# Spacing of the weight conversions in the gated MLP's second pass, and two ordering edges

## The chip, the cores and the metric

The kernel runs on one core of a Trainium2 chip. The metric is the device time of one execution in microseconds (us), taken as the median of several. TensorE (PE) multiplies, with its weight loads shown as PEld; ScalarE (ACT) and VectorE (DVE) do the elementwise work; SyncE (SP) issues nearly all transfers. Each of these engines runs its own instruction list in order. PSUM holds matmul results in eight banks, SBUF holds everything else.

## The reference

```python
attn_out = _attn_ref(q, k, v)          # causal window of 64, 4 x 8 heads x 576 tokens x 64
x = attn_out.transpose(0, 2, 1, 3).reshape(2304, 512)
# gated MLP: 512 -> 1536 -> 512
xn = x / np.sqrt(np.mean(x * x, axis=-1, keepdims=True) + 1e-6) * rms_g
g = xn @ w_gate
x2 = g / (1 + np.exp(-g)) * (xn @ w_val) @ w_out
# second MLP: 512 -> 2048 -> 512
h = x2 @ w_in2
out = h / (1 + np.exp(-1.702 * h)) @ w_out2
```

The weights arrive as 64-bit floats, and the kernel makes 32-bit floats of them itself.

## The kernel before

**Stages.** The 2304 tokens are six blocks of 384. A first pass goes over the six blocks with the first half of the hidden columns of the gated MLP, and does the attention of later blocks in between. A second pass goes over three super-blocks (`sb` 0 to 2) of two blocks with the other half of the hidden columns. Then comes the second MLP, the gelu stage. Each float32 matmul is done as three matmuls on a high and a low part.

**The second pass.** A matrix product of it is a Winograd scheme: seven products of half size for each pair of blocks. One hidden column pair makes one `chain` (line 1020) of seven steps; a step (`prod`) is six matmuls with 384 columns. There are six chains in a super-block, n even for the gate and n odd for the value. A chain works in two PSUM banks, a and b. Steps 0, 1 and 2 each end with `snap` (line 1038), a copy of the bank to SBUF on ACT; steps 3, 4 and 5 end with `plus`, an addition on DVE; step 6 is read from its bank. Later steps go on in the same bank, so that PE may begin step 2 only when the copy of step 0 is done, step 3 when that of step 1 is done, and step 4 when that of step 2 is done. The results go through `gated` (line 1265, Silu on ACT) or `valued` (line 1269, a product on DVE, a cast on ACT at line 1273, the low part on DVE at line 1274). After the chains, `out_units` multiply with the output weights and add to what the first pass left.

**Order.** PE's order is written out by hand. In the second pass each piece of work has a key; super-block `sb` begins at key 50·sb, chain n of it has its steps at keys 7n, 7n+2, ..., 7n+12, and from key 7 on two chains alternate, so that one key is about one step. In the first pass, pieces hang on a count of matmuls (`at_tick`). ACT, DVE and SP are not ordered by hand: a planner with a simulated clock places their instructions, by order of the source among those that it takes to be ready, and may place them well ahead of the work around them. `with after(ins)` adds an edge: what the block issues on the engine of `ins` stands behind `ins`. `hold[0]` is the ACT instruction, `hold_v[0]` the DVE instruction, that was noted last.

**Conversions.** `w_order` lists pairs of weight tiles. Six gate and value pairs of the second half are converted in the first pass by `conversion()` (line 1117); then come three pairs of output weights ("o"), eight pairs of the second MLP's first matrix ("h", all wanted in the gelu stage) and eight of its second ("p"). The "o" and "h" pairs are converted in the second pass by `w_step` (line 240): two ACT instructions on the loaded tile `st` (lines 253 and 254, behind `hold[0]`), two on DVE (255 and 256), then the load of the next pair (`w_load`, line 135). The following `w_step`, or a `w_half` at its own key, finishes the pair: an "o" is split into high and low part (lines 236 and 237); an "h" gets four differences (206 to 209), the high part on ACT (214), the low part on DVE (216) and two stores to DRAM (225, 226). The pool `stp` has three slots of 8 KB a partition for `st` and for the result `m`.

**Transfers.** All go through SP's one queue: weight tiles of a chain (`t_load`, line 1012, 896 KB each, two a chain, the tile freed by an earlier chain), the pairs to be converted (1 MB), the stores of converted pairs, and the next super-block's input (`x_raws`, line 983). `x_steps` (line 986) makes the seven operands `xop` of a super-block out of that input (DVE 1001, ACT 1003, DVE 1004), seven pieces at keys 48.05 and up.

Of the kernel before, what the change touches and what calls it, by code (L numbers as in the profile page):

```python
# [9 lines left out]
F32 = mybir.dt.float32  # L10
# [31 lines left out]
def window_attention__gated_mlp__mlp_kernel(  # L42
# [554 lines left out]
    if True:  # L597
# [382 lines left out]
        def x_raws(src):  # L980
            r = [wp.tile([128, KC, TB], F32, tag="w", name="xr") for _ in range(2)]
            for e in range(2):
                nc.sync.dma_start(out=r[e], in_=src(e))
            return r

        def x_steps(r, ops, hold_on=()):
            a11, a12, a21, a22 = r[0][:, 0:2, :], r[0][:, 2:4, :], r[1][:, 0:2, :], r[1][:, 2:4, :]
            subs = [
                (0, None, a11), (6, (a21, a11, a21, ALU.subtract), a21), (5, (a21, a22, a21, ALU.subtract), a21),
                (4, (a11, a11, a21, ALU.add), a11), (2, (a21, a12, a21, ALU.subtract), a21), (1, None, a12), (3, None, a22),  # L990
            ]

            def step(i, total, src):
                with ExitStack() as es:
                    for ins in hold_on:
                        es.enter_context(after(ins))
                    make(i, total, src)

            def make(i, total, src):
                if total:  # L1000
                    nc.vector.tensor_tensor(*total)  # L1001
                t = x1p.tile([128, 2, 2, TB], F32R, tag="xop", name="xop")
                nc.scalar.copy(t[:, 0], src)  # L1003
                nc.vector.tensor_tensor(t[:, 1], src, t[:, 0].bitcast(F32), ALU.subtract)
                ops[i] = t

            return [lambda a=a: step(*a) for a in subs]

        def t_load(key):
            w = [wp.tile([128, 7, 256], F32R, tag="w", name="wt") for _ in range(2)]  # L1010
# [9 lines left out]
        def chain(n, load, ops, take):  # L1020
            w, xo = load(), ops

            def prod(ps, i, first):
                k = 0
                for wi, xi in ((0, 0), (1, 0), (0, 1)):
                    for c in range(2):
                        on_pe(
                            nc.tensor.matmul,
                            ps[:, :TB],
                            w[wi][:, W_OF["g"][i], c * 128:(c + 1) * 128],  # L1030
                            xo[i][:, xi, c, :],
                            start=(first and k == 0),
                            stop=(k == 5),
                            skip_group_check=not first,
                        )
                        k += 1

            def snap(ps):
                t = small("sn")
                nc.scalar.copy(t, ps[:, :TB])  # L1040
                return t

            def plus(t, ps):
                nc.vector.tensor_tensor(t, t, ps[:, :TB], ALU.add)  # L1044
                return t

            a = bank(n, 0)
            prod(a, 0, True)
            s1 = snap(a)
            yield  # L1050
            b = bank(n, 1)
            prod(b, 6, True)
            s7 = snap(b)
            yield
            prod(a, 5, False)
            s2 = snap(a)
            yield
            prod(b, 3, False)
            take(2, plus(s2, b))
            yield  # L1060
            prod(a, 4, False)
            take(3, plus(s7, a))
            yield
            b = bank(n, 1)
            prod(b, 1, True)
            take(0, plus(s1, b))
            yield
            prod(a, 2, False)
            take(1, a[:, :TB])
            yield  # L1070
# [3 lines left out]
        def put(key, fn):  # L1074
            items.append((key, len(items), fn))
# [32 lines left out]
        def evict(j, acc):  # L1108
            for c in range(KC):
# [4 lines left out]
                    nc.scalar.mul(st, acc[c][:, :T], 0.5)  # L1114
                nc.sync.dma_start(out=osd[j // 2][:, c, (j % 2) * TB:(j % 2 + 1) * TB], in_=st)

        def conversion():
            env = {}

            def first():  # L1120
                w_load(w_next[1] + 1)
                env["key"] = w_order[w_next[1]][0]
                w_next[1] += 1
                st = staged.pop(0).rearrange("p e (f two) -> p (e f) two", two=2)
                env["lo"], env["up"] = lo, hi = st[:, :, 0], st[:, :, 1]
                with after(hold[0]):
                    nc.scalar.activation(hi.bitcast(F32), hi.bitcast(F32), AF.Prelu, scale=2.0 ** -112, alpha=-(2.0 ** 32))

            def second():
                lo, hi = env["lo"], env["up"]  # L1130
                env["mt"] = mt = stp.tile([128, 2, 1024], I32, tag="st", name="m")
                with after(hold[0]):
                    nc.scalar.activation(lo, lo.bitcast(U32), AF.Copy, scale=2.0 ** -29)
                with after(hold_v[0]):
                    nc.vector.tensor_scalar(mt[:, 1, :].bitcast(U32), hi.bitcast(U32), 3, None, ALU.logical_shift_left)

            def add():
                m = env["mt"][:, 1, :]
                with after(hold_v[0]):
                    nc.vector.tensor_tensor(m, m, env["lo"], ALU.add)  # L1140
                with after(last_hop[0]):
                    w_load(w_next[1] + 1)

            def differences():
                env["t"] = t = env["mt"].bitcast(F32).rearrange("p e (b c) -> p (e b) c", c=256)
                b11, b21, b22, b12 = (t[:, 4 + i] for i in range(4))
                with after(hold_v[0]):
                    nc.vector.tensor_tensor(t[:, 0], b12, b11, ALU.subtract)
                    nc.vector.tensor_tensor(t[:, 1], b22, t[:, 0], ALU.subtract)
                    nc.vector.tensor_tensor(t[:, 2], b22, b12, ALU.subtract)  # L1150
                    nc.vector.tensor_tensor(t[:, 3], b21, t[:, 1], ALU.subtract)

            def upper(a, b):
                if a == 0:
                    env["hi"] = wp.tile([128, 7, 256], F32R, tag="w", name="whi")
                with after(hold[0]):
                    nc.scalar.copy(env["hi"][:, a:b], env["t"][:, a:b])

            def lower(a, b):
                hi, m = env["hi"][:, a:b], env["t"][:, a:b]  # L1160
                with after(hold_v[0]):
                    nc.vector.tensor_tensor(m.bitcast(F32R), m, hi.bitcast(F32), ALU.subtract)
                if b == 7:
                    key = env["key"]
                    d = dram.tile([128, 2, 7, 256], F32, name="w%s_%d" % key, tag="w%s_%d" % key)
                    wd[key] = d
                    with after(last_hop[0]):
                        nc.sync.dma_start(out=d[:, 0], in_=env["hi"].bitcast(F32))
                        nc.sync.dma_start(out=d[:, 1], in_=env["t"][:, 0:7])

            return [
                first, second, add, differences,
                lambda: upper(0, 4), lambda: lower(0, 4), lambda: upper(4, 7), lambda: lower(4, 7),
            ]

        for pieces in [[462,474,480,512,516,522,524,529],[562,574,582,588,678,683,687,693],[728,736,743,778,782,788,792,798],[894,900,906,910,942,946,950,954],[959,964,970,976,982,988,992,998],[1004,1010,1016,1022,1034,1040,1044,1048]]:
            for t, fn in zip(pieces, conversion()):
                at_tick(t, fn)
        evict(0, accs)
# [81 lines left out]
        def gated_chains(sb):  # L1261
# [7 lines left out]
            def valued(p, q, c):  # L1269
                t = a4[p, q]  # L1270
                nc.vector.tensor_tensor(t, t, c, ALU.mult)
                g[p, q] = u = gp.tile([128, 2, TB], F32R, tag="g", name="g")
                nc.scalar.copy(u[:, 0], t)
                nc.vector.tensor_tensor(u[:, 1], t, u[:, 0].bitcast(F32), ALU.subtract)

            for i, p in enumerate(ZIG[sb]):
                for k, fn in enumerate((gated, valued)):
# [46 lines left out]
        def put_units(start, units, room):  # L1324
# [3 lines left out]
                key += n if key >= room[0] and key < room[1] else 2  # L1328
            return key

        for sb in range(NSB):
            chains, g = gated_chains(sb)
            put_chains(t0, chains)
            for at_key in [[2.5, 10, 17.5, 25, -32], [6, 16, 26, -36], [2.5, 11, 20, 29, -36]][sb]:
                put(t0 + abs(at_key), w_half if at_key < 0 else lambda: w_step(n_wi))
            for i, (n, fn) in enumerate(out_units(sb, g)):
                if i < 3:
                    key = t0 + 42.2 + 2 * i
# [6 lines left out]
            all_ops[sb + 1] = nops  # L1345
            nsrc = (lambda e, sb=sb: xd[2 * sb + 2 + e]) if sb + 1 < NSB else (lambda e: x2d[0][:, :, e * TB:(e + 1) * TB])
            box = []
            put(t0 + 36.5, lambda nsrc=nsrc, nops=nops, box=box: box.extend(x_steps(x_raws(nsrc), nops)))
            for i in range(7):
                put(t0 + 48.05 + 0.1 * i, lambda box=box: box.pop(0)())  # L1350
            if sb + 1 == NSB:
# [238 lines left out]
```

## Time and profile before

| | |
|---|---|
| three runs | 907.08, 908.44, 909.31 us, median 908.44 |
| the profiled execution | 909.66 us, of which 907.9 us from first to last instruction |
| TensorE clock granted | 1.000 on average |
| PE busy | 898.5 us of 907.9 |
| second pass | from about 328 to 540 us |

The span is what the rows below measure; the 1.8 us around it belong to the execution and stand in every time. A matmul's end is modelled, so PE's progress is read from the starts of its groups.

### The profile page before, as it was taken

How to read it: one execution, taken by the hardware profiler on the slowest of the kernel's cores; microseconds unless marked ns; L12 is line 12 of the kernel's file. 1: busy time of each engine (PE TensorE's matmuls, PEld its weight loads, DVE VectorE, ACT ScalarE, POOL GpSimd, SP SyncE). 2: the span in 40 equal slices, each digit the busy share in tenths (PEclk: the TensorE clock that was granted, in tenths of full speed). 3: DMA queues.
4: the chain of work that ended last, by engine and by line, in shares of the span. 5: the costliest groups of instructions: out<-in, count | busy, mean ns of one | idle time of the engine just before them, and what ended most of it. 6: DMA issues, size and time to landing. Idle time of an engine off the chain costs nothing.

```text
span 907.9 us, 16654 instructions
## 1 busy us (share of the span) xinstructions
PE 898.5 (99%) x6458; PEld 867.5 (96%) x6458; DVE 602.8 (66%) x1237; ACT 509.3 (56%) x1026; POOL 12.9 (1%) x39
## 2 busy tenths in 40 slices
PE   9999999999999999999999999999999999999998
PEld 8999999999999999999999998889899999999998
DVE  5998657777688747937867896656633488234753
ACT  6896656646475356626726657565545455245442
POOL 2000000000000000000000000000000000000000
PEclk9999999999999999999999999999999999999999
DMA  9987576978958859559889989898697778767851
GB/s 205 244 246 216 167 186 197 257 215 236 285 169 312 320 200 344 193 199 376 336 269 354 389 310 381 315 329 294 203 354 263 278 285 310 249 250 262 324 204 53
DMA packets 159407, 240.04 MB, mean 264 GB/s; under 512 B 81248, under 2 KB 131424, under 8 KB 155744
## 3 DMA queue, kind: packets, MB, share of 16 engines
q1 hardware_dynamic: 158800, 238.97, 79.0%
q8 instruction: 51, 0.84, 0.4%
q14 instruction: 28, 0.23, 0.1%
q10 hardware_dynamic: 528, 0.00, 0.0%
HBM read 167.64 MB, written 59.24 MB: 250 GB/s over the span
## 4 chain that ended last, share of the span: by engine, by line
PE 87%; DMA 4%; DVE 4%; ACT 3%; issue 1%; SPq 0%; ACTq 0%; DVEq 0%
PE acc L115 21%; PE psa L115 17%; PE psb L115 13%; PE acca L115 7%; PE psg L115 6%; PE psv L115 5%; PE accb L115 5%; PE ps_warm L121 2%; PE psg L121 1%; PE acc L121 1%; PE psv L121 1%; DMA xr<-x 1%; DMA st<-in_moe_w_in_dram 1%; PE ps_v L115 1%; PE ps_s L115 1%
## 5 line engine op out<-in xcount | busy, mean ns | idle before, releaser
L115 PE MATMUL psa<-xop,wt 128*128 128x384 f32 x1008 | 192.8, 335 | 0.7 <-ACT sn L1040 0.7
L115 PEld LDWEIGHTS psa<-xop,wt 128*128 128x128 f32 x1008 | 176.5, 188 | 3.8 <-ACT sn L1040 1.1
L115 PE MATMUL psb<-xop,wt 128*128 128x384 f32 x756 | 147.2, 335 | 2.7 <-ACT sn L1040 2.4
L115 PEld LDWEIGHTS psb<-xop,wt 128*128 128x128 f32 x756 | 132.5, 188 | 5.7 <-ACT sn L1040 3.0
L1044 DVE TENSOR_TENSOR sn<-sn,psb 128x384 f32<-128x384 f32 x84 | 46.2, 550 | 69.9 <-PE psb L115 68.6
L115 PE MATMUL acc<-g,w 128*128 128x384 f32 x432 | 78.1, 334 | 0.0
L115 PEld LDWEIGHTS acc<-g,w 128*128 128x128 f32 x432 | 75.2, 188 | 0.0
L115 PE MATMUL acca<-wo,sop 128*128 128x256 f32 x576 | 72.0, 283 | 0.3 <-DVE sop L1398 0.3
L1398 DVE TENSOR_TENSOR sop<-g,sop 128x768 fp32r<-128x768 f32 x56 | 53.3, 957 | 28.5 <-ACT sop L1397 28.3
L115 PEld LDWEIGHTS acca<-wo,sop 128*128 128x128 f32 x576 | 70.8, 191 | 0.5 <-DVE sop L1398 0.5
L1040 ACT COPY sn<-psa 128x384 f32<-128x384 f32 x84 | 40.0, 477 | 55.6 <-PE psa L115 55.6
L1397 ACT CAST sop<-g 128x768 fp32r<-128x768 f32 x56 | 46.5, 838 | 40.5 <-PE accb L115 21.7
L115 PE MATMUL acc<-whi,g 128*128 128x512 f32 x192 | 67.8, 392 | 0.0
L1374 ACT ACTIVATE g<-sn 128x384 f32<-128x384 f32 x48 | 25.3, 527 | 52.1 <-DVE sn L1044 52.1
L115 PE MATMUL accb<-wo,sop 128*128 128x256 f32 x432 | 52.8, 283 | 0.0
L115 PEld LDWEIGHTS accb<-wo,sop 128*128 128x128 f32 x432 | 52.3, 192 | 0.0
L1003 ACT CAST xop<-xr 128x768 fp32r<-128x768 f32 x42 | 34.0, 836 | 30.8 <-DVE xr L1001 25.8
L115 PE MATMUL acc<-ah,w 128*128 128x384 f32 x240 | 50.8, 342 | 0.0
L115 PE MATMUL psg<-xh,w 128*128 128x384 f32 x240 | 50.1, 342 | 0.6 <-DVE a L1205 0.5
L115 PE MATMUL psv<-xh,w 128*128 128x384 f32 x240 | 50.3, 340 | 0.0
L420 ACT ACTIVATE p<-p,sm 128x128 f32<-128x128 f32 x96 | 37.5, 393 | 17.1 <-DVE sm L408 17.1
L115 PEld LDWEIGHTS psg<-xh,w 128*128 128x128 f32 x240 | 41.4, 188 | 2.3 <-DVE a L1205 1.2
(204 smaller groups left out, 1565.0 us busy)
## 6 DMA issues: line engine op xcount, KB each, us to landing
wt<-wh SPq DMA_DIRECT2D x48, 896.0 KB, 6.5
wo<-wp SPq DMA_DIRECT2D x28, 1024.0 KB, 6.8
st<-in_moe_w_out_dram SPq DMA_DIRECT2D x28, 512.0 KB, 8.1
wt<-wg SPq DMA_DIRECT2D x14, 896.0 KB, 7.4
wt<-wv SPq DMA_DIRECT2D x14, 896.0 KB, 8.2
xr<-x SPq DMA_DIRECT2D x12, 768.0 KB, 7.2
wh<-whi SPq DMA_DIRECT2D x8, 896.0 KB, 8.3
wh<-m SPq DMA_DIRECT2D x8, 896.0 KB, 9.9
```

The lines of the kernel that those rows point to most:

```text
L115: ins = op(*args, **kw)
L121: ins = op(*args, **kw)
L420: last_exp[0] = nc.scalar.activation(p[e][:, hp, :], p[e][:, hp, :], AF.Exp, bias=sm[:, 0, i:i + 1], scale=-1.0, accum_out=sm[:, 1, i:i + ...
L1003: nc.scalar.copy(t[:, 0], src)
L1040: nc.scalar.copy(t, ps[:, :TB])
L1044: nc.vector.tensor_tensor(t, t, ps[:, :TB], ALU.add)
L1374: hold[0] = nc.scalar.activation(g[pg, q][:, j % 2], c, AF.Gelu_apprx_sigmoid).ins
L1397: nc.scalar.copy(t[:, 0], src)
L1398: nc.vector.tensor_tensor(t[:, 1], src, t[:, 0].bitcast(F32), ALU.subtract)
```

## The change

The first pair of output weights is converted in the last block of the first pass (pieces at ticks 1130, 1142, 1150 and 1240). The remaining ten conversions of the second pass are at keys 2.5, 13.5 and 24.5 in super-block 0 (before: 2.5, 10, 17.5 and 25), at 4, 15 and 26 in super-block 1 (before: 6, 16 and 26), and as before in super-block 2; the closing `w_half` of super-block 0 moves from key 32 to 33. `snap` notes its copy in `hold[0]`, so a conversion's ACT instructions stand behind the last copy in the source, where before they stood behind the last Silu. `valued` notes its last subtraction in `hold_v[0]`, and pieces 2 to 6 of the second pass's `x_steps` issue their DVE instructions behind it.

```diff
-        def x_steps(r, ops, hold_on=()):
+        def x_steps(r, ops, hold_on=(), held_from=7):
...
-            return [lambda a=a: step(*a) for a in subs]
+            def held(a):
+                with after(hold_v[0]):
+                    step(*a)
+
+            return [lambda a=a, n=n: held(a) if n >= held_from else step(*a) for n, a in enumerate(subs)]
...
             def snap(ps):
                 t = small("sn")
-                nc.scalar.copy(t, ps[:, :TB])
+                hold[0] = nc.scalar.copy(t, ps[:, :TB]).ins
                 return t
...
+        n_made = [0]
+
         def conversion():
             env = {}
 
             def first():
                 w_load(w_next[1] + 1)
+                env["pair"] = w_order[w_next[1]]
                 env["key"] = w_order[w_next[1]][0]
...
+            if w_order[w_next[1] + n_made[0]][0][0] == "o":
+                def keep():
+                    half.append((env["pair"], env["mt"][:, 1, :]))
+                    with after(hold[0]), after(hold_v[0]):
+                        w_half()
+
+                return [first, second, add, keep]
+            n_made[0] += 1
             return [
...
-        for pieces in [...,[1004,1010,1016,1022,1034,1040,1044,1048]]:
+        for pieces in [...,[1004,1010,1016,1022,1034,1040,1044,1048],[1130,1142,1150,1240]]:
...
-                nc.vector.tensor_tensor(u[:, 1], t, u[:, 0].bitcast(F32), ALU.subtract)
+                hold_v[0] = nc.vector.tensor_tensor(u[:, 1], t, u[:, 0].bitcast(F32), ALU.subtract).ins
...
+        W_STEPS = ((2.5,13.5,24.5),(4,15,26),(2.5,11,20,29))
+        W_LAST = (33,36,36)
         for sb in range(NSB):
             chains, g = gated_chains(sb)
             put_chains(t0, chains)
-            for at_key in [[2.5, 10, 17.5, 25, -32], [6, 16, 26, -36], [2.5, 11, 20, 29, -36]][sb]:
-                put(t0 + abs(at_key), w_half if at_key < 0 else lambda: w_step(n_wi))
+            for at_key in W_STEPS[sb]:
+                put(t0 + at_key, lambda: w_step(n_wi))
+            put(t0 + W_LAST[sb], w_half)
...
-            put(t0 + 36.5, lambda nsrc=nsrc, nops=nops, box=box: box.extend(x_steps(x_raws(nsrc), nops)))
+            put(t0 + 36.5, lambda nsrc=nsrc, nops=nops, box=box: box.extend(x_steps(x_raws(nsrc), nops, held_from=2)))
```

## Rows read from the trace of the kernel before

**Rows 1.** The profile page: busy us, share of the span and instructions of each engine

```profile
PE 898.5 (99%) x6458; PEld 867.5 (96%) x6458; DVE 602.8 (66%) x1237; ACT 509.3 (56%) x1026; POOL 12.9 (1%) x39
```

**Rows 2.** Waits, second pass: who waited for whom, us in total, times, longest

```profile
ACT st L253 <- DMA st<-in_moe_w_in_dram: 7.6, 4, 3.4
...
PEld psb L115 <- ACT sn L1040: 3.0, 2, 1.7
...
PEld psa L115 <- ACT sn L1040: 1.1, 1, 1.1
```

**Rows 3.** Timeline near 362 us: start, us, engine, line, what, [idle before]

```profile
360.47 2.24 PE L115 MATMUL psa<-xop,wt 128*128 128x384 f32 x12
361.10 1.14 ACT L253 ACTIVATE st<-st 128x1024 f32<-128x1024 f32 x1 [2.60 <-DMA st<-in_moe_w_in_dram]
...
363.20 0.45 ACT L1040 COPY sn<-psb 128x384 f32<-128x384 f32 x1
...
363.71 1.32 PE L115 MATMUL psb<-xop,wt 128*128 128x384 f32 x6 [0.99 <-ACT sn L1040]
```

**Rows 4.** Timeline near 415 us, super-block 1

```profile
413.75 2.24 PE L115 MATMUL psb<-xop,wt 128*128 128x384 f32 x12
414.12 1.17 ACT L253 ACTIVATE st<-st 128x1024 f32<-128x1024 f32 x1 [1.40 <-DMA st<-in_moe_w_in_dram]
...
416.73 2.38 PE L115 MATMUL psa<-xop,wt 128*128 128x384 f32 x12 [0.74 <-ACT sn L1040]
```

**Rows 5.** Timeline near 495 us, super-block 2

```profile
492.79 2.24 PE L115 MATMUL psa<-xop,wt 128*128 128x384 f32 x12
493.82 1.13 ACT L253 ACTIVATE st<-st 128x1024 f32<-128x1024 f32 x1 [3.37 <-DMA st<-in_moe_w_in_dram]
...
496.42 1.33 PE L115 MATMUL psb<-xop,wt 128*128 128x384 f32 x6 [1.38 <-ACT sn L1040]
```

**Rows 6.** Timeline at 332 us, start of super-block 0

```profile
332.36 1.20 PE L115 MATMUL psa<-xop,wt 128*128 128x384 f32 x6
332.71 0.48 ACT L1040 COPY sn<-psb 128x384 f32<-128x384 f32 x1
333.40 1.23 PE L115 MATMUL psb<-xop,wt 128*128 128x384 f32 x6
```

**Rows 7.** Timeline: super-block 2's first conversion (two rows), a low part, chain 5's start

```profile
448.03 1.15 ACT L253 ACTIVATE st<-st 128x1024 f32<-128x1024 f32 x1
...
452.79 1.23 DVE L256 CUSTOM_DVE_ANT_0 m<-st,m 128x2048 uint16<-128x2048 uint16 x1
...
502.23 2.03 DVE L216 TENSOR_TENSOR m<-m,whi 128x1792 fp32r<-128x1792 f32 x1 [1.21 <-ACT whi L214]
...
504.88 2.28 PE L115 MATMUL psa<-xop,wt 128*128 128x384 f32 x12
```

**Rows 8.** Two transfers by line: issues (ns, first and last start), then landing times

```profile
L135 SPq DMA_DIRECT2D st<-in_moe_w_in_dram x3: 383/468/499, 454.0 to 455.0; - x3
...
DMA to landing us min/median/max: 4.1/4.4/4.6
...
L1012 SPq DMA_DIRECT2D wt<-wv x1: 320/320/320, 494.7 to 494.7; - x1
...
DMA to landing us min/median/max: 9.9/9.9/9.9
```

**Rows 9.** Stretches: us, busy PE, PEld, DVE, ACT, POOL (count), clock, DMA share, GB/s

```profile
442.00:465.90 23.90, 23.90 (x139) 23.90 (x139) 23.00 (x33) 11.27 (x15) 0.00 (x0) 1.00 0.68 231
...
474.20:512.40 38.20, 36.82 (x213) 36.44 (x212) 26.59 (x47) 23.84 (x43) 0.00 (x0) 1.00 1.00 373
```

**Rows 10.** Timeline at the end of the second pass: next operands, first gelu product

```profile
526.83 0.55 DVE L1274 TENSOR_TENSOR g<-a,g 128x384 fp32r<-128x384 f32 x1
...
531.02 2.68 DVE L1004 TENSOR_TENSOR xop<-xr,xop 128x768 fp32r<-128x768 f32 x3
...
540.28 1.20 PE L115 MATMUL psa<-xop,wt 128*128 128x384 f32 x6
```

More of the change, by code (lines that the diff above doesn't have):

```diff
@@ L1174, in conversion @@
             ]
-        for pieces in [[462,474,480,512,516,522,524,529],[562,574,582,588,678,683,687,693],[728,736,743,778,782,788,792,798],[894,900,906,910,942,946,950,954],[959,964,970,976,982,988,992,998],[1004,1010,1016,1022,1034,1040,1044,1048]]:
+        for pieces in [[462,474,480,512,516,522,524,529],[562,574,582,588,678,683,687,693],[728,736,743,778,782,788,792,798],[894,900,906,910,942,946,950,954],[959,964,970,976,982,988,992,998],[1004,1010,1016,1022,1034,1040,1044,1048],[1130,1142,1150,1240]]:
             for t, fn in zip(pieces, conversion()):
```

## The prediction

> **What bounds the kernel now.** I read the page first, then the waits, then the timeline around each wait, then transfers. PE is busy for 898.5 of 907.9 us, and neither DVE (66%) nor ACT (56%) comes near it [rows 1]. So the time is PE's work plus the few places where PE stops, and a change that leaves the matmuls alone can win only those stops. In the second pass, which this change is about, the list of waits holds three stops worth speaking of, all for the copy of a product bank: 3.0 + 1.1 = 4.1 us of waiting weight loads [rows 2].
>
> The timeline shows that the copy is not the cause. PE's pace is a step of six matmuls in 1.04 us (333.40 − 332.36) [rows 6], so a group of twelve takes 2.08. Near 362 us, the group that began at 360.47 should have been followed at 362.55; the next began at 363.71, **1.16** late [rows 3]. It waited for a copy that ran only at 363.20, because ACT stood in the first instruction of a conversion (line 253) with nothing to do for 2.60 us, until its data had landed at 361.1; then the conversion's two instructions took until 363.20. The copy, whose bank had been full for a good while, stood behind them. By the same reckoning the stop near 415 us is 416.73 − 415.83 = **0.90** [rows 4] and that near 495 us 496.42 − 494.87 = **1.55** [rows 5]. Sum 3.61 us; the waits view gives 4.1 as a bound, as it counts the restart too. The reader should see one pattern three times: a load that lands late, an ACT instruction placed as if it had landed, a copy behind it. A fourth conversion waited for its load as well (four waits, 7.6 us [rows 2]: 2.60 + 1.40 + 3.37 leave 0.2) and cost PE nothing, as no copy was due.
>
> **Super-block 0.** Taking one "o" pair out leaves three conversions at a distance of 11 keys, 11 × 1.04 = 11.4 us, where 7.5 keys were 7.8 us. The load of a pair is issued only when the conversion before it has gone through its first instructions, so the distance has to hold those, some 2 to 3.5 us, and the load. The parts of one pair land in 4.1 to 4.6 us each in a light queue, and a tile under load in 9.9 [rows 8]: 6 to 13 us in all. 7.8 us lies at the lower end, 11.4 near the upper, so I take it that the 1.16 goes. What comes instead: the first conversion now stands behind the copy at 332.71 (step 1), where before it ran ahead of the chains. Its two ACT instructions take 363.20 − 361.10 = 2.1 us [rows 3]; behind 333.2 they end at 335.3, and the copy of step 2, 0.45 long, at 335.75. PE wants that bank two steps after 333.40, at 335.48 [rows 6]. I charge **+0.25** (bounds: 0, if the removed split of the pair lets the copy run earlier; 0.9, if one more ACT instruction of about that length goes in between). Super-block 0: −1.16 + 0.25 = −0.91.
>
> **First pass.** It gains two ACT instructions (2.1 us together [rows 3]), their DVE partners, one split on each engine, and the issue of one load on SP ahead of the chains' tiles. No row of before shows it there. PE has 99% there as elsewhere, and each bank has one step group of slack, so I charge 0; between −0.1 and +0.6, the last from one copy behind the 2.1 us less its slack.
>
> **Super-block 1.** The first conversion moves from key 6 to 4, the second from 16 to 15. Its pair has long landed; the load of the next is issued right behind it. So that load starts some 2 us or more earlier (two keys), against a conversion that starts at most 1 earlier, and the wait of 1.40 us on ACT [rows 4] has about 1 to 3 us more room. I take the whole stop: **−0.90** (bounds −1.1 and 0).
>
> **Super-block 2.** Its keys are unchanged, its place is not. Before, the first conversion ran at 448.03 [rows 7], 18 us ahead of its super-block, among the output units: only an old Silu stood before it. Now it stands behind the copy of step 1. Chain 5's start at 504.88 [rows 7] is key 135; 28 steps of 1.04 and the stop before it, key 107 began at 474.2; six steps earlier, as output units lie between, is step 1 of chain 0, at 468.0, and its copy is done at about 469.5. The following load, its four differences, high part and low part (2.03 us [rows 7]) and two stores come later by as much. In 442 to 466 us the transfers filled 0.68 of the time and ACT 11.27 of 23.9 us; in 474 to 512 us the transfers filled 1.00, at 373 GB/s, and DVE 26.59 of 38.2 us [rows 9]. So work moves from a stretch with room to one whose queue is full. DVE has the room: 2.03 for the low part, 1.23 for the second instruction on `st` and, as an estimate from these by size, 2.3 for the rest [rows 7] make 5.6 us more, 84% of 38.2. The load that PE waited for at 493.8 is issued behind the conversion of key 111, 478.4 by the same count, which stays; I expect it to land at 492 to 494 as before. If 492, the copy behind it is in time. But behind this stop there is another: chain 5 began at 504.88, and its second weight tile, issued at 494.7 and landed 9.9 us later, at 504.6 [rows 7, 8]. It is wanted at the third matmul, 0.35 us into the chain. Without the stop of 1.55 PE is there at 503.33 + 0.35 = 503.68 and waits 0.9 for the tile. So of 1.55 at most 0.7 comes back: **−0.70** (bounds: −1.55, if the tile lands earlier because two stores have left the queue ahead of it; +5, rival three).
>
> **The held operands.** Pieces 2 to 6 now follow the last subtraction of `valued`, at 526.83 in super-block 2. Before, the last operand was done at 531.02 + 2.68 = 533.70, and PE wanted the first at 540.28 [rows 10]: 6.6 us of cover. From 527.4 on the held pieces need three additions or subtractions and five low parts on DVE, 8 × 0.95, about 7.6 us, so 535 to 537. Charged at nothing; if the cover were gone it would cost what passes 540.3, not over 2 us. In the other two super-blocks the same work ends against the same start of the next chain. The gain of it, that `valued` isn't pushed back on DVE, frees PE from nothing that the waits show.
>
> **The sum** is −0.91 − 0.90 − 0.70 = −2.5 us. Against the profiled execution's 909.66 that is 907.15; that execution lies 1.2 us above the median, so on the median of 908.44 the forecast is **905.9**, −0.28%.
>
> **A rule against this.** A part of a pair took 4.4 us to land at 454 and a tile 9.9 us at 494.7 [rows 8], where the transfers were busy throughout [rows 9]: the second was queueing. The Trainium skill, "DMA: Bandwidth & Descriptors", section "Queues, rings and completion order", says that SP's transfers go down one ring on each DMA engine, and that descriptors are consumed in ring order. By that rule whatever is moved ahead of a chain's tile delays it by its own bytes, and the second super-block's wider spacing buys nothing in super-block 2, where the ring never empties. That is rival three's mechanism.
>
> **Rivals.**
> *One: all three stops go.* The loads land in time everywhere and chain 5's tile arrives earlier, since the two stores of super-block 2's first pair leave the queue ahead of 474 us. Then 908.44 − 4.1 = **904.3**. For it: the queue before 474 us gets lighter. Against: share 1.00 behind it [rows 9].
> *Two: the stops only move.* The planner still places line 253 by its own idea of when a load lands, and a conversion 2 us later or earlier meets another copy. Two of three stops remain at their mean of 1.2, with 0.25 in super-block 0: 908.44 − 1.2 + 0.25 = **907.5**, within 0.5 of no change. For it: one conversion in four waited without harm, which is luck and not spacing [rows 2].
> *Three: slower; the queue in super-block 2.* The stores of the moved pair (2 × 0.92 MB, at 373 GB/s 4.9 us [rows 9]) and the 1 MB load behind it (2.8 us) are issued after 477 us, ahead of the tiles of chains 3 to 5. Tiles come late by up to 7.7 us, less the 1 or 2 us that the queue is empty before. Chain 5 would wait 0.9 + 6, where 1.55 was: 908.44 − 1.8 + 5.3 = **911.9**. It decides by whether the stores are issued before the tiles at about 480; they are not held and DVE has the room, so I think they are.
> *Four: nothing of it happens,* as the planner had other reasons for its order: 908.4; counted with two.
>
> **How the numbers follow.** Forecast 0.40, one 0.28, two with four 0.20, three 0.12. About 0.3% is what a measurement of this kernel can tell from no change: 2.7 us, so the borders are 905.7 and 911.2. One is faster; of the forecast, whose own range is 904.9 to 906.9, some 0.35; faster 0.28 + 0.14 = 0.42. Three gives slower 0.11. Same 0.47. The range reaches from one's time to past two's, 904.0 to 909.6, and leaves three out.
>
> **What would show it.** Right: no wait of PE for line 1040 near 362 and 415; the first conversion of super-block 0 just behind the copy at 333 with a short wait there; that of super-block 2 near 469.5 instead of 448; a wait of chain 5 for a tile (`wt`) of under 1 us. Rival three shows as waits of PE for `wt` in 480 to 510 that sum to over 2 us; rival two as waits for line 1040 at other places, each with line 253 and a transfer before it. The prediction is wrong if PE stops outside the second pass by a microsecond more than before, or in the first pass behind the added conversion.

## The result, and the profile after

The changed kernel takes **916.8 us** (median of five runs, 914.46 to 918.04) against 908.93 for the kernel before (five runs): ratio 1.0085, 95% interval 1.0067 to 1.0104. That is slower by 7.9 us, where 905.9 was forecast and 909.6 was the end of the range.

The profiled execution took 914.46 us, its span is 912.7. The page after, its span and its busy times, which answer to [rows 1]:

```profile
span 912.7 us, 16657 instructions
...
PE 899.3 (99%) x6458; PEld 867.3 (95%) x6458; DVE 604.8 (66%) x1237; ACT 509.3 (56%) x1026; POOL 12.9 (1%) x39
```

Each engine has as many instructions as before, and PE (+0.8 us) and DVE (+2.0 us) are busy for nearly as long. What differs is what PE waits for. The waits of PE over the whole run, in the columns of [rows 2]:

```profile
PE psa L115 <- DMA wt<-wv: 4.3, 3, 2.7
PE psa L115 <- DMA wt<-wg: 2.7, 1, 2.7
```

The copies of product banks (line 1040 before, 1044 now) are gone from this list: the three stops on which the prediction was built have all disappeared. In their place stand four waits for a chain's weight tile, 7.0 us, which the kernel before had nowhere. The timeline shows the three long ones, one in super-block 1 and two in super-block 2:

```profile
429.48 2.02 PE L115 MATMUL psa<-xop,wt 128*128 128x384 f32 x10 [2.66 <-DMA wt<-wg]
...
493.87 2.01 PE L115 MATMUL psa<-xop,wt 128*128 128x384 f32 x10 [2.74 <-DMA wt<-wv]
...
510.16 2.02 PE L115 MATMUL psa<-xop,wt 128*128 128x384 f32 x10 [1.20 <-DMA wt<-wv]
```

PE runs the same 6458 matmuls in the same order in both kernels, so each one's start can be set against its own start before. The distance between the two executions changes at these places, and hardly anywhere else:

| place (time in the kernel after) | distance changes by | what it is |
|---|---|---|
| up to 297 | +0.5 | a wait of 0.7 at 284 that is new, a shorter one at 297 |
| 337 | +0.15 | the late copy of step 2, super-block 0 |
| 363 | −1.3 | stop of [rows 3] gone |
| 415 | −1.0 | stop of [rows 4] gone |
| 419 and 429 | +0.6 and +3.0 | tiles of chains 3 and 4, super-block 1 |
| 494 | +3.0 | tile of chain 3, super-block 2 |
| 500 | −1.4 | stop of [rows 5] gone |
| 510 | +1.5 | tile of chain 5, super-block 2 |
| 754 | −0.2 | a shorter wait in the gelu stage |
| end | +4.8 in all | |

So the profiled execution lost 4.8 us against that of the kernel before, 4.5 of them in the second pass. The medians differ by 7.9: the profiled execution before lay 0.7 above its median, the one after 2.3 below (916.8 − 914.46). Those 2.3 go with the granted clock: 1.000 in the profiled execution, 0.994 to 0.996 in the four others, 916.3 to 918.0 us; the section on the hardware comes back to it.

Why the tiles were late in super-block 2 is read from SP's list. These lines of the timeline follow the first pair of super-block 2 and the tile that PE waited for (SPq is SP's issue of a transfer):

```profile
471.48 1.16 ACT L253 ACTIVATE st<-st 128x1024 f32<-128x1024 f32 x1
...
479.45 2.02 DVE L216 TENSOR_TENSOR m<-m,whi 128x1792 fp32r<-128x1792 f32 x1 [0.57 <-ACT whi L214]
...
482.08 0.80 SPq L1327 DMA_DIRECT2D part<-o  x2
482.98 0.38 SPq L225 DMA_DIRECT2D wh<-whi  x1
...
483.45 0.38 SPq L226 DMA_DIRECT2D wh<-m  x1
483.92 0.73 SPq L1016 DMA_DIRECT2D wt<-wv  x1
```

The conversion began at 471.48 and not at 448.03 [rows 7]. Its two stores were issued at 482.98 and 483.45, right ahead of chain 3's tile at 483.92; the tile landed 9.9 us later, at 493.8, and PE had come to it at 491.1. Before, the tile was issued at 480.6, behind four `part` transfers and no store of a pair later than 467.0, and landed 7.9 us later, at 488.6. The stretches of [rows 9], now, and a piece of the last one:

```profile
442.00:465.90 23.90, 23.90 (x140) 23.90 (x139) 18.11 (x28) 8.08 (x13) 0.00 (x0) 1.00 0.56 204
465.90:474.20 8.30, 8.30 (x50) 8.30 (x49) 2.30 (x4) 3.41 (x5) 0.00 (x0) 1.00 0.69 253
474.20:512.40 38.20, 34.25 (x195) 33.27 (x194) 29.57 (x52) 22.21 (x38) 0.00 (x0) 1.00 0.95 348
...
482.00:484.00 2.00, 2.00 (x13) 2.00 (x12) 0.96 (x2) 2.00 (x3) 0.00 (x0) 1.00 0.35 111
```

From 442 to 466 us the transfers fell from 0.68 to 0.56 of the time and DVE from 23.0 to 18.1 us: the room there is left unused. From 474 on they fill 0.95 of the time, with a hole at 482 to 484, where the stores begin. SP had stood at a load of `part` (line 1327), which had to wait until the stores of earlier parts (line 1331) had landed:

```profile
SPq L1327 <- DMA x<-part: 4.9, 2, 4.3
```

The long one of these two waits ended at 482.08. The store it waited for had been issued at 476.6 and landed at 482.07, behind the next pair's load (issued from 473.87 on, landed by 481.0), which before had gone out at 454 [rows 8]. So what the moved conversion brings stands in SP's way twice: first its load, then its stores.

### The profile page after: what moved, and what is told of

The parts are those of the page before. It is cut to its first block, busy times and chain, and to the rows that moved or that the text cites. A ratio compares the mean times of both kernels' runs of the same rounds, so it can differ in the third digit from the quotient of the medians.

```text
span 912.7 us, 16657 instructions
## 1 busy us (share of the span) xinstructions
PE 899.3 (99%) x6458; PEld 867.3 (95%) x6458; DVE 604.8 (66%) x1237; ACT 509.3 (56%) x1026; POOL 12.9 (1%) x39
## 4 chain that ended last, share of the span: by engine, by line
PE 87%; DMA 7%; DVE 3%; ACT 2%; issue 1%; SPq 0%; ACTq 0%; DVEq 0%
PE acc L115 21%; PE psa L115 18%; PE psb L115 13%; PE acca L115 7%; PE psg L115 6%; PE psv L115 5%; PE accb L115 5%; DMA wt<-wv 2%; PE ps_warm L121 1%; PE psg L121 1%; PE acc L121 1%; PE psv L121 1%; DMA wt<-wg 1%; DMA xr<-x 1%; PE ps_v L115 1%; PE ps_s L115 1%
## 5 line engine op out<-in xcount | busy, mean ns | idle before, releaser
L1004 DVE TENSOR_TENSOR xop<-xr,xop 128x768 fp32r<-128x768 f32 x42 | 39.2, 952 | 6.7 <-ACT xop L1003 6.6
```

## The experiments

Two theories were set against each other first. *The queue*: conversion traffic stands ahead of the chains' tiles in SP's one list, because of where the conversions begin. *The held operands*: DVE work behind the last subtraction delays the chains and so the freeing of tile slots. Times are medians, and each ratio is to runs of the kernel before of its own group (median 908.0 for the first four experiments, 908.1 for the second four, 909.3 for the next three, 907.5 for the last).

### Without the note of the copy

```diff
-                hold[0] = nc.scalar.copy(t, ps[:, :TB]).ins
+                nc.scalar.copy(t, ps[:, :TB])
```

> The changed kernel without the note of the product-bank copy (snap sets no hold). Theory, the queue: the changed kernel lost because transfers of the conversions (loads of the next pair, stores of the finished one) stand ahead of the chains' tiles in SP's one list. Without the note the first conversion of super-block 2 runs before 460 us again, its stores leave before 475, and PE's waits for tiles in super-block 2 (3.0 and 1.5 us) fall below 1.5 in sum; the 2.96 us near 426 stay; the stop for line 1044's copy near 495 may come back (1.5). Time 910.5 to 913.5. Rival, the held operands: DVE work held behind the last subtraction delays the chains and with them the freeing of tiles; then super-block 2 keeps over 3 us of waits for tiles and the time stays at 915 to 918.

**906.9 us**, ratio 0.9989 (0.9970 to 1.0008), less than expected. All waits for tiles went, that near 426 as well, which had been expected to stay; and no stop behind a late load came back. The first conversions of super-blocks 1 and 2 began here:

```profile
372.12 1.14 ACT L253 ACTIVATE st<-st 128x1024 f32<-128x1024 f32 x1
...
441.12 1.13 ACT L253 ACTIVATE st<-st 128x1024 f32<-128x1024 f32 x1
```

29 and 30 us earlier than with the note (401.2 and 471.5). Without this one line the whole loss is gone. For super-block 1 that isn't the place of the kernel before, where the first conversion, at key 6, ran behind the first Silu of its own super-block:

```profile
404.21 0.53 ACT L1267 ACTIVATE sn<-sn 128x384 f32<-128x384 f32 x1 [2.26 <-DVE sn L1044]
404.64 1.12 ACT L253 ACTIVATE st<-st 128x1024 f32<-128x1024 f32 x1
```

The held operands are still in this kernel, so the rival falls for the loss of the change.

### Super-block 1 at its old keys

```diff
-        W_STEPS = ((2.5,13.5,24.5),(4,15,26),(2.5,11,20,29))
+        W_STEPS = ((2.5,13.5,24.5),(6,16,26),(2.5,11,20,29))
```

> The changed kernel with super-block 1's conversions at keys 6, 16 and 26 as before. Queue theory: the load of the third pair of super-block 1 is issued behind chain 4's tile again, the wait of 2.96 us near 426 goes, the stop of 0.9 us behind a late load comes back or not; super-block 2 as in the changed kernel. Time 913 to 915.5. Rival, the held operands: the wait near 426 has another cause and stays, 916 to 918.

**914.3 us** (1.0069, 1.0044 to 1.0093). The wait near 426 fell from 2.7 to 0.9; super-block 2 kept its long wait, 3.1, but not the one for chain 5's tile. Two keys less lead put the next pair's load (419.6) behind chain 4's tile (418.1) again; in the changed kernel two of its three parts went out at 416.2 and 416.7, ahead of that tile at 417.3, which then took 12.2 us to land where it had taken 6.9 before. That is as the queue theory has it, but the wait did not go altogether, as had been expected: the tile still took 9.8 us. The stores of the pair before it moved by 1.5 to 2.0 us as well; which of the two, loads or stores, made the tile late was not separated.

### Operands not held

```diff
-... box.extend(x_steps(x_raws(nsrc), nops, held_from=2))
+... box.extend(x_steps(x_raws(nsrc), nops))
```

> The changed kernel with x_steps not held behind the last subtraction. Queue theory: DVE has room, so the waits for tiles stay near 7 us in sum, 915.5 to 918. Rival, the held operands: they fall by half or more, 911 to 914.

**917.2 us** (1.0089, 1.0061 to 1.0117). The waits for tiles are 4.2 + 2.7 us, as in the changed kernel. The held operands do not cause them.

### Stores from another engine's queue

```diff
+        eng = nc.gpsimd if kind == "h" else nc.sync
-        nc.sync.dma_start(out=dst[0], in_=hi[:, 0:7].bitcast(F32))
+        eng.dma_start(out=dst[0], in_=hi[:, 0:7].bitcast(F32))
```

(and the second store likewise)

> The changed kernel with the two stores of each second-MLP pair issued from GpSimd's queue instead of SP's. Queue theory, order in SP's list: the tiles of chains 3 to 5 of super-block 2 no longer stand behind two stores; PE's waits for tiles in super-block 2 fall from 4.5 to under 2 us and the time to 911 to 914.5. Rival, bytes alone: the transfers are saturated from 474 us on, the same bytes have to move before the tiles, and the waits stay above 3.5 us, 915.5 to 918.

**919.0 us** (1.0116, 1.0083 to 1.0150). The wait at 491 did go, and one of 3.4 at 498, for chain 4's tile, came; super-block 2 has 3.4 in all, where 3.9 was. The other three waits are in super-block 1 (1.3, 0.5 and 1.5, near 419, 428 and 436), whose stores moved too. PE's waits for tiles over the run:

```profile
PE psa L115 <- DMA wt<-wg: 3.9, 2, 3.4
PE psa L115 <- DMA wt<-wv: 2.8, 2, 1.5
```

and the last stretch of [rows 9] in this kernel, in the same columns:

```profile
474.20:512.40 38.20, 34.79 (x187) 34.47 (x186) 26.93 (x49) 21.16 (x36) 2.31 (x5) 0.91 0.99 358
```

The sum of the waits, 6.7, is nearly that of the changed kernel (7.0), and the transfers fill 0.99 of the stretch. So SP's list is where the lateness shows, and taking the stores out of it doesn't make room for their bytes. The two stores issued on GpSimd's queue at 491.5 and 494.1, after chain 4's tile (489.7), landed at 501.5 and 505.8, the tile at 502.1. The rival, bytes alone, is nearer: it had over 3.5 us in super-block 2 and 915.5 to 918, where the queue theory had under 2 and at most 914.5.

### The note alone

```diff
 # the kernel before, with
-                nc.scalar.copy(t, ps[:, :TB])
+                hold[0] = nc.scalar.copy(t, ps[:, :TB]).ins
```

> The kernel before with one line of the change: snap notes its copy in hold[0]. Theory, the note: by itself it keeps the first conversion of super-block 2 until about 469 us and so puts that pair's stores and the following load ahead of the chains' tiles; PE waits 3 to 5 us for tiles in super-block 2, the stops near 362 and 415 stay. Time 911 to 915. Rival, keys and first pass: the note harms only together with the moved keys; 907 to 909.5.

**917.1 us** (1.0112, 1.0097 to 1.0127), more than expected. The stops near 362 and 415 went, other than expected; the wait for a tile is 2.1 where 3 to 5 were expected, and others came:

```profile
PE acc L115 <- DVE g L1274: 2.5, 1, 2.5
PE psa L115 <- ACT sn L1040: 2.2, 2, 1.8
PE psa L115 <- DMA wt<-wv: 2.1, 1, 2.1
```

The note alone costs what the whole change costs, and not by tiles alone: near 525 PE waits for a subtraction of `valued` that stands behind operand pieces and a pair's low part on DVE. That wait is not in the changed kernel, where the operands are held, but nor is it in the changed kernel without the hold, so the hold alone doesn't explain it. The wait of 1.8 for a product bank is at 557, in the gelu stage; its cause was not looked for.

### First pass and super-block 0 alone

```diff
 # the changed kernel, with
-        W_STEPS = ((2.5,13.5,24.5),(4,15,26),(2.5,11,20,29))
+        W_STEPS = ((2.5,13.5,24.5),(6,16,26),(2.5,11,20,29))
 # and without the note and without held_from=2
```

> The kernel before with the conversion in the first pass and super-block 0 at keys 2.5, 13.5, 24.5 and 33 alone: no note of the copy, operands not held, super-block 1 at its old keys. Theory, the note: no wait for tiles above 0.5 us in the second pass; the stop of 1.2 us near 362 goes; those near 415 and 495 (0.9 and 1.6) stay, as their conversions have their old keys. Time 906.5 to 908.5. Rival, keys and first pass: waits for tiles of 3 us or more, over 911.

**908.3 us** (1.0010, 1.0001 to 1.0019). No wait for a tile. The stop near 362 went (1.16); those near 415 and 495 shrank by 0.3 and 0.7. The timed runs show no gain from it.

### Fewer bytes

```diff
+        if kind == "h" and p >= 4:
+            return
         nc.sync.dma_start(out=dst[0], in_=hi[:, 0:7].bitcast(F32))
 # and t_load takes the tiles of the first four pairs in their place
```

> The changed kernel without the stores of the last four second-MLP pairs (7.3 MB; the gelu stage loads the first four pairs' tiles in their place, so that part of the second MLP uses wrong weights); every instruction of PE, ACT and DVE stays. Theory, saturated transfers: with those bytes gone the tiles of super-block 2 land in time, the waits of 3.0 and 1.5 us there fall below 0.5 together, the wait of 3.0 near 426 stays; 909.5 to 913. Rival, late freeing of the tiles by the chains: the waits stay over 3 us, 915 to 918.

**913.1 us** (1.0070, 1.0049 to 1.0091). No wait for a tile is left in super-block 2, and 2.6 near 426. The transfers' share from 474 to 512 us is 0.85. But the time came down by only 3.7 us: a late load and a copy behind it stop PE again, and PE waits 1.4 near 297 and 1.0 near 529, which it doesn't in the changed kernel.

```profile
495.99 1.14 ACT L255 ACTIVATE st<-st 128x1024 f32<-128x1024 f32 x1 [3.92 <-DMA st<-in_moe_w_in_dram]
...
498.57 1.31 PE L115 MATMUL psb<-xop,wt 128*128 128x384 f32 x6 [1.90 <-ACT sn L1046]
```

(Lines 255 and 1046 are this kernel's 253 and 1044.) With the run on GpSimd's queue it shows that the stores' bytes made the tiles of super-block 2 late, and not SP's stop at the `part` load: that stop lasts until 482.1 here and 482.8 there, and in both chain 3's tile is in time. Once the tiles are in time, the old stop is back.

### Without the note, operand pieces of the first pass behind a cast

```diff
                         if todo:
-                            todo.pop(0)()
+                            with after(hold[0]):
+                                todo.pop(0)()
```

> The changed kernel without the note of the copy, and with the operand pieces of the first pass's last block behind the latest ACT instruction there (hold[0]), so that the cast that waits for the input's transfer doesn't stand before the tanh. Theory: the stop near 297 us, 0.6 us in the kernel before and up to 1.9 in the first experiments, falls to under 0.2; no waits for tiles in the second pass; 905 to 906.5, below both kernels. Rival: the stop is DVE's and stays, 906.5 to 907.5.

**906.2 us** (0.9983, 0.9974 to 0.9993). This is about the stop near 297 us, which is in the kernel before as well and varied between the kernels (0.6 late before, 0.3 after; waits of 1.2 to 1.8 in some experiments). It is the same pattern as the three stops: a cast waits for the input's transfer, the tanh behind it is late, and PE waits for its bank. With the pieces held the stop is gone. A wait of 1.1 for a tile near 433 took part of it back.

### The first conversions early, the note kept

```diff
-        W_STEPS = ((2.5,13.5,24.5),(4,15,26),(2.5,11,20,29))
+        W_STEPS = ((2.5,13.5,24.5),(4,15,26),(-8,11,20,29))
```

> The changed kernel, note of the copy and held operands kept, with super-block 2's first conversion at key 92 (8 before the super-block's first key, among the output units) instead of 102.5. Theory, place: the note harms only by where it lets this conversion begin; it then begins before 455 us, PE's waits for tiles in super-block 2 fall from 4.5 to under 1.5 us, that of 3.0 near 426 stays; 909.5 to 913. Rival, the edge itself (other conversions kept late by it): the waits in super-block 2 stay over 3 us, 915 to 918.

**910.8 us** (1.0020, 1.0005 to 1.0035). Super-block 2's first conversion began at 444.4; no wait for a tile is left there, and 2.4 us near 426. As expected.

```diff
+        W_STEPS = ((2.5,13.5,24.5),(-8,15,26),(-8,11,20,29))
```

> As the last, and super-block 1's first conversion at key 42 instead of 54 too. Theory, place: no waits for tiles over 1 us in the second pass, with the note and the held operands in the kernel; 905.5 to 908, the time of the changed kernel without the note. Rival, the edge itself: over 911.

**906.3 us** (0.9966, 0.9953 to 0.9978). The complete list of PE's waits of this kernel:

```profile
PE psg L115 <- DVE a L1220: 1.6, 1, 1.6
PE ps_v L605 <- DVE QT L602: 1.4, 1, 1.4
PE psb L115 <- ACT a L1514: 0.3, 1, 0.3
PE acca L115 <- DVE sop L1416: 0.3, 1, 0.3
```

Nothing of the second pass is in it. The note as such does no harm; two keys that it made binding did. Super-block 2's first conversion (441.6) is back near its old place (448.0); that of super-block 1 (373.7) is in a new one, 31 us ahead of the old.

```diff
 # and the operand pieces of the first pass held, as above
```

> The last one with the operand pieces of the first pass's last block behind the latest ACT instruction there. If both places are what cost the time, this is faster than both kernels: 905 to 906.8; the stop near 297 us under 0.2. If waits for tiles remain in super-block 1 or 2, 907 to 909.

**905.7 us** (0.9962, 0.9950 to 0.9975), the fastest of all, below both kernels; its profiled span is 903.6. The stop near 297 is gone.

### The same without the held operands

```diff
 # both first conversions early, the note kept, held_from=2 left out
```

> The kernel with both first conversions early (keys 42 and 92) and the note of the copy, without the held operands. If the held operands are worth something by themselves, the last subtractions of valued come later, PE waits for them (line of the low part of g) by 0.5 to 2.5 us near 520 to 530, and the time is 907 to 909. If not, no such wait and 905.5 to 907.

**911.9 us** (1.0049, 1.0028 to 1.0069), more than the 907 to 909 expected, and 5.6 more than with them (by the two ratios, 7.5). PE waits 2.2 us for DVE's last subtractions:

```profile
PE acc L115 <- DVE g L1289: 2.2, 1, 2.2
```

The wait ends at 386.8 us, in super-block 0, and is not near 520 as expected: the conversion that now begins among the output units meets the operand pieces there on DVE. The granted clock is 0.50 for some 3 us behind it; the rest of the difference is not traced. So holding the operands, which is worth nothing in the changed kernel, is needed once the conversions begin early with the note in place.

## Why the prediction was wrong

**What bounds the kernel** was read rightly, and so were the causes of the three stops: all three went, for −1.3, −1.0 and −1.4 us in the profiled execution (1.16, 0.90 and 1.55 were reckoned).

**Super-block 0**: −0.91 forecast, −1.1 measured. The conversion stands behind the copy of step 1, as worked out, and the +0.25 for the late copy measures 0.15 to 0.2: the group that should take 2.24 takes 2.42. The wider spacing did what was expected: the two conversions after it, at 342.05 and 355.09, wait for no load.

```profile
333.08 0.48 ACT L1044 COPY sn<-psb 128x384 f32<-128x384 f32 x1 [0.69 <-PE psb L115]
333.46 1.14 ACT L253 ACTIVATE st<-st 128x1024 f32<-128x1024 f32 x1
...
334.96 2.42 PE L115 MATMUL psa<-xop,wt 128*128 128x384 f32 x12
```

**First pass**: charged at nothing, and PE has no wait between 297 and 328 us, where the added conversion is. The +0.5 of the table lies ahead of it.

**Super-block 1**: −0.90 forecast, −1.0 + 0.6 + 3.0 = +2.6 measured. The gain came as forecast: the load behind the first conversion went out at 402.1 where it had been 407.9, and the second conversion waited for nothing. The step that failed is that "that load starts some 2 us or more earlier" was booked as pure gain. Earlier conversions make every load earlier, and it was not asked what stood behind them. The load behind the second conversion passed chain 4's tile in SP's list. Before:

```profile
418.80 0.32 SPq L1012 DMA_DIRECT2D wt<-wg  x1
...
420.06 2.21 SPq L135 DMA_DIRECT2D st<-in_moe_w_in_dram  x3
```

and after:

```profile
416.24 0.94 SPq L135 DMA_DIRECT2D st<-in_moe_w_in_dram  x2
417.26 0.53 SPq L1016 DMA_DIRECT2D wt<-wg  x1
```

PE waited 2.7 us for the tile; at the old keys the wait is 0.9. The bounds given, −1.1 and 0, left a loss out without a reason.

**Super-block 2**: −0.70 forecast, −1.4 + 3.0 + 1.5 = +3.1 measured. The conversion began at 471.5, which is the forecast's 469.5 and the 2.0 us lost by then. The place was named (rival three, "the stores of the moved pair … are issued … ahead of the tiles of chains 3 to 5"), the bounds went to +5, and the wait of chain 5 was 1.2 to 1.5 where 0.9 was reckoned. The step that failed is the choice within these bounds: "They are not held and DVE has the room, so I think they are" issued before the tile at 480. They weren't. The low part was done at 481.5, and SP's list stood at a `part` transfer until 482.08 in any case. The prediction went through DVE's room and not through SP's order, though [rows 9] had the transfers at 1.00. The −1.4 was in part luck: the load behind this stop was expected at 492 to 494 and landed at 497.6 to 499.0, and in the run with fewer bytes, where its last part landed at 495.9 and PE was less late, the stop is there with 1.9 us. Rival three gave 911.9; the profiled executions, 4.8 us apart, make 913.2 of the forecast's 908.44. That this rival got 0.12 was the larger error: moving transfers into a stretch that [rows 9] show at 1.00 was no place to expect a gain.

**The held operands** were charged at nothing, and in this change they cost and gave nothing that the runs show (917.2 without them). What they are for shows where conversions begin early.

**The clock** had no term at all. The 2.3 us between the profiled execution and the median are put down to it by the mean clocks; there is no trace of the four other executions that would show it. A stop can also cost more than it lasts, as the last section shows.

**The rule against the change** held: "DMA: Bandwidth & Descriptors" of the Trainium skill ("Queues, rings and completion order") has descriptors consumed in ring order. The trace agrees in this stretch: issued at 482.98, 483.45 and 483.92, the two stores and the tile landed 4.4, 7.0 and 9.9 us later, at 487.4, 490.5 and 493.8, one after the other. The same page's section "Issuing engines are not separate DMA queues" says that DMAs started by different engines run on the same 16 DMA engines and interleave. The run with the stores on GpSimd's queue agrees: 919.0 us, and 6.7 us of waits for tiles where 7.0 were.

## What to carry to other kernels

Before moving work that issues transfers, write down the transfer list of the place it goes to, and ask which tile will stand behind it; here stops of 1.0 to 1.4 us were traded for waits of 2.7 us behind that list. An edge that keeps an instruction from running too early also keeps it from running in a gap many microseconds ahead: check where each of the instructions under it ran before, and give those that used a gap a place of their own there. And what an edit is worth can hang on the others: here the note of the copy, early first conversions and held operands make 906.3, while leaving out the second gives 916.8 and leaving out the third 911.9. That the note itself is needed is not shown: the changed kernel without it takes 906.9.

## What the hardware showed that I had not expected

PE's clock can fall behind a single stop of 3 us. In the run with super-block 1 at its old keys PE stood for 3.1 us before 492.8. The stretches before and after it, with the granted clock as the column before the last two:

```profile
488.00:492.70 4.70, 1.69 (x10) 1.37 (x8) 4.25 (x7) 2.62 (x4) 0.00 (x0) 1.00 0.97 359
492.80:496.00 3.20, 3.20 (x10) 3.20 (x11) 0.07 (x1) 0.48 (x1) 0.00 (x0) 0.50 1.06 374
496.00:500.00 4.00, 4.00 (x25) 4.00 (x24) 1.75 (x3) 2.59 (x4) 0.00 (x0) 0.99 1.03 410
```

For 3.2 us the granted clock is 0.50, the lower of its two levels (1.2 of 2.4 GHz), and PE starts 10 matmuls where 18 fit, so the stop costs some 1.5 us more than it lasts. The changed kernel's profiled execution has a stop of 2.7 us at the same place and kept its clock:

```profile
493.90:497.00 3.10, 3.10 (x18) 3.10 (x19) 0.96 (x2) 0.53 (x2) 0.00 (x0) 1.00 1.09 375
```

Its other four executions have a mean clock of 0.994 to 0.996, against 1.000 in nearly all of the kernel before, and take 1.8 to 3.6 us more than the profiled one (916.3 to 918.0 less 914.46). In the run at super-block 1's old keys the one spell goes with a mean clock of 0.998. In the run with the note alone, at 0.996, there are two, behind stops of 2.1 and 1.8 us:

```profile
489.80:493.10 3.30, 3.30 (x13) 3.30 (x12) 1.08 (x3) 0.48 (x1) 0.00 (x0) 0.50 1.05 363
558.10:561.40 3.30, 3.30 (x10) 2.82 (x9) 3.29 (x4) 0.48 (x1) 0.00 (x0) 0.50 1.10 384
```

By that, 0.996 would be two spells and 0.994 three, as an estimate 3.0 and 4.5 us, against the 1.8 to 2.9 and the 3.6 measured, so such spells would be enough; where they lie in those executions no trace shows. What decides whether a stop of that length brings the clock down was not tried. "TensorE: Matmul & The Clock Gate" of the Trainium skill describes the mechanism (section "HAM oscillation — how this bites in real kernels": a wait for a transfer throttles PE, and the next work starts cold); the stretches at 492.80 and 489.80 agree, each behind a wait for a tile, and the one at 1.00 is behind a wait of 2.7 us for a tile that did not bring it.
